# Split experts of a fused attention, gating and expert kernel: 32-bit parts, and scaled 16-bit parts with guards

## The chip, the cores and the metric

The kernel runs on one core of one Trainium2 chip. The metric is device time in microseconds (us) of one execution; of several runs the median is taken. A profile of one execution names the engines: PE is the matrix engine, PEld its loading of the stationary operand, DVE, ACT and POOL are the vector, scalar and general engines, and SP issues most of the DMAs.

## What is computed

Three stages follow one another: a linear attention with a decaying state (4 batches, 8 heads, 768 steps, 48 values), a dense stage with a gated soft activation and a layer norm (384 to 1024 to 384), and eight experts of which each token uses one.

```python
# stage 3, of which the change speaks: x is 3072 tokens by 384
logits = x @ w_gate                       # 8 experts
expert_idx = np.argmax(logits, axis=1)
gate_w = softmax(logits)[np.arange(N), expert_idx]
for e in range(8):
    mask = expert_idx == e
    h = np.maximum(x[mask] @ w1[e], 0.0)  # 384 to 1024
    out[mask] = gate_w[mask, None] * (h @ w2[e])   # 1024 to 384
```

## The kernel before

The tokens go in 24 tiles of 128. Each tile passes the attention (`square` to `yout`) and the dense stage (`ysquare` to `mm2`); then its rows are sent by an indirect DMA to the place of its expert in `xs` (`xrow`, `choose`, `gexp`, `gate`, `rank`, `place`, `send`). When nearly all tiles are sent, the experts run one after the other, each over as many rows as it may have: 480 (in two parts of 256 and 224 rows, y = 0 and 1, of the expert that leads after 15 tiles), then 464, 432, 416, 400, 384, 368 and 344.

Precision is kept by splitting: each operand is a high part and the rest, and three matmuls (high by high, high by rest, rest by high) stand for one. Of the attention's and the dense stage's second matmul the parts are 16 bits wide (`mm2`, line 567). Of the experts all parts are 32 bits wide (type F32R): the rows (`ehi` on ACT, `elo` on DVE, line 773 and 776), the weights (line 724 on ACT, 726 on DVE) and the inner values (`rhi` on ACT, line 800, `rlo` on DVE, line 803).

For one expert of n rows `emm1` (line 789) makes 72 matmuls of n columns, in four quarters of 18. After each quarter ACT takes the result to the high part (`hh`) and DVE to the rest (`hl`); the results stand in two large PSUM banks, so the third quarter needs the first one's bank back. The second layer is 72 matmuls of n columns where n is over 384 (`emm2t`, line 832), else 24 matmuls of 384 columns for each 128 rows (`emm2`, line 814). The two parts of the first expert have 72 matmuls each in `emm1` and 48 each in `emm2`. That is 648 matmuls at line 789, 288 at line 832 and 312 at line 814, together 1248. Between them stand 87 transposes of rows (`etrans`, line 770).

An expert's weights come in four chunks (1024, 512, 768 and 768 KB) through two staging buffers (`stage`, loads at line 717), and each chunk is split by ACT and DVE from there.

The order of the work is not written by hand: `plan()` takes every step with its engine, its cost and a due time from the table `X`, and always issues the step that can start first, among those within `EPS` of it the one with the lowest due time. Each engine then works through its own list strictly in that order. The steps of `tables()` (powers of the decay, needed by all attention steps) and the memsets around them stand ahead of that stretch and are ordered by the framework's scheduler.

At the end `marks`, `flags` and `judge` decide whether a slow path is needed (values out of the range that the split allows, or an expert with too many rows): `flags` is a small matmul, `judge` a chain on DVE whose last line (692) writes `fli`. All engines read `fli` (line 1206) and jump past the slow path.

Of the kernel before, what the change touches and what calls it, by code (L numbers as in the profile page):

```python
# [23 lines left out]
P = 128  # L24
# [9 lines left out]
NOID = 4095  # L34
SA, SV, SZ, SW = 2.0 ** 10, 2.0 ** 9, 2.0 ** 8, 2.0 ** 10
# [5 lines left out]
def body(ctx, tc, r, k, v, w, u, w_in, w_out, g_ln, w_gate, w1, w2, out):  # L41
# [18 lines left out]
    def sml(name, slot=None):  # L60
# [25 lines left out]
    X = dict(PK=14, ET=-29.23, GG=-120.46, SO=-383.87, FL=374.6, OL=1, ybuf=10, tmp=1, rkv=3, LAT=0.06,  # L86
             SELF=0.05, PRE=1.4, EPS=0.1, TA=176.56, TB=248.64, TM=254.17, NA=8, NB=9, M0=495.42, W0=42.93,
             TW=105, W1=-530.44, TV=257.99, PF=664.51, PW=-382.4, F0=-386.07, EL=3, e=3, S0=12.3, P0=10.1,
             D0=2.5, L0=-679.5, L1=615.58, U0=13.12, KG=9.92, PT=2, ZT=-247.56, F2=148.59, TE=84.91, GA=118.81,
             GW=-220.86, GN=157.31, DB=-1.5, KS=8.04, K0=610.2, K1=199.94, xtrans=-970.71, kev=571.15,  # L90
             ahi=622.76, vlo=9.17, ruk=307.19, attend=625.35, choose=-170.33, xhi=-20.99, vhi=706.01,
             own=263.22, hvar=668.67, hmax=132.27, gexp=-753.32, ktrans=-390.29, rtrans=539.68, hexp=150.63,
             ztrans=70.39, asum=173.22, rev=-2168.6, xlo=-650.67, decay=77.28, alo=655.25, rank=-472.96,
             ld=-228.91, xrow=-249.65, mm2=1203.62, causal=-107.84, hseed=-596.66, send=-284.2, hsolu=-201.28,
             yout=597.49, zlo=288.89, scores=540.82, square=141.08, place=-51.35, ysquare=-575.28,
             advance=-342.55, update=136.08, zscale=-399.78, hroot=-622.85, mm1=452.87, aval=631.76,
             kpow=460.49)
# [26 lines left out]
    thr = const.tile([P, 1], F32, name="thr")  # L124
    ph1 = ctx.enter_context(ExitStack())
# [447 lines left out]

    def choose(i):
# [100 lines left out]
    def judge():  # L675
# [15 lines left out]
        V.tensor_tensor(fl[:, 1:2], fl[:, 1:2], fl[:, 0:1], op=ALU.max)  # L691
        V.tensor_copy(fli[:, 1:2], fl[:, 1:2])
# [4 lines left out]
    wts = {}  # L697

    def weights(e):
# [3 lines left out]
        def pair(m):  # L703
            if m not in tiles:
                shape = [P, KD, FF] if m == 1 else [P, KF, DM]
                tiles[m] = [(wb if e % 2 else wa).tile(shape, F32R, name=f"w{m}{x}", tag=f"w{m}{x}") for x in "hl"]
            return tiles[m]

        def chunk(m, c0, n, width):
# [19 lines left out]
            return lambda part: split() if part else load()  # L729
# [3 lines left out]
    cv, sto, gt, wg, mxp = fold_pools(pha, "")  # L733
    tables()
# [29 lines left out]
    def etrans(d, c, slot=None):  # L764
        if c == 0:
            d["xh"] = d["new"]([P, KD, d["mx"]], F32R, "exh")[:, :, 0:d["nr"]]
            d["xl"] = d["new"]([P, KD, d["mx"]], F32R, "exl")[:, :, 0:d["nr"]]
# [161 lines left out]
    for i in range(NT):  # L929
# [49 lines left out]
        op(("choose", i), "", [("dve", .18), ("dve", .27), ("dve", .24), ("pool", .25)], [("mm2", i), ("send", i - 3), "wos"], choose, i, first=f + X["choose"])  # L979
        op(("xrow", i), "act", .58, [("mm2", i), ("send", i - 3), ("fill", E - 1), "wos"], xrow, i, first=f + X["xrow"])  # L980
# [28 lines left out]
    for y in range(E + 1):  # L1009
        e, d = max(y - 1, 0), {}  # L1010
        if y == 2:
            esends.clear()
        if y != 1:
# [4 lines left out]
            for n, (m, w_) in enumerate(((2, FF), (1, FF), (4, DM), (4, DM))):  # L1018
                op(("wload", e, n), "dma", m * w_ * 4 * P / 230e3, [("yout", NT - 1), ("who", 0)] + [("who", e), ("wlo", e, n - 2) if n > 1 else ("wlo", e - 1, n + 2), ("wload", e, n - 1) if n else ("wload", e - 1, 3)],
# [4 lines left out]
                   lambda g=wz[n]: g(1), first=f + X["GN"] * n)  # L1024
        f = start[y]
# [334 lines left out]
```

## Time and profile before

| what | value |
|---|---|
| median of 3 runs | 625.04 us (624.47 to 629.82) |
| the profiled execution's own time | 626.75 us |
| its span in the trace | 624.9 us |
[...]
| busy PE, PEld, DVE | 91%, 78%, 71% |
| busy ACT, POOL | 57%, 41% |

Times in the trace count from the span's start. "Busy" of PE holds the modelled end of each matmul, so that matmuls that follow closely show as one busy stretch; the pace is read from the distance between their starts. The chain of work that ended last is followed backwards from the last instruction, each piece to what released it.

### The profile page before, as it was taken

To read this page: it belongs to the slowest core of one execution; us is meant where nothing else is said; L and a number is where in the kernel's file an instruction comes from. 1 tells how busy PE (TensorE), PEld (TensorE's weight loads), DVE (VectorE), ACT (ScalarE), POOL (GpSimd) and SP (SyncE) were. 2 spreads that over 40 slices of the span, in tenths; PEclk is the share of its full clock that TensorE was granted. 3 is DMA by queue.
4 is the path that set the end of the run, shared out by engine and by line. 5 is a ranking of instruction groups with operands and counts; after the bars stand their busy time and mean duration, and the time that the engine had idled before them with its cause. 6 is when DMAs were issued, how large, how long until landed. Compare 5 with 4: busy or idle time off the path is not lost. (4 is left out here: it accounts for less than half of the span.)

```text
span 624.9 us, 10949 instructions
## 1 busy us (share of the span) xinstructions
PE 568.8 (91%) x4035; PEld 488.3 (78%) x4035; DVE 442.5 (71%) x781; ACT 354.8 (57%) x590; POOL 258.0 (41%) x427
## 2 busy tenths in 40 slices
PE   0757798999999999999999989999999999999990
PEld 0646687677777788878787658988899999989990
DVE  5899989978898989989877653537576767546211
ACT  2556677597688768678577762535252525345310
POOL 1687567365655646766543452110012121212210
PEclk9968799899999999999999999999999999999996
DMA  9736459794647475745324724853546585763100
GB/s 174 164 92 147 96 171 305 93 188 86 124 93 134 83 116 104 124 86 104 63 47 130 194 71 154 278 173 111 158 129 204 146 236 162 144 193 132 52 14 25
DMA packets 159872, 82.80 MB, mean 132 GB/s; under 512 B 136917, under 2 KB 153034, under 8 KB 159424
## 3 DMA queue, kind: packets, MB, share of 16 engines
q1 hardware_dynamic: 156544, 72.53, 50.9%
q0 software_dynamic: 3264, 9.47, 4.5%
q8 instruction: 34, 0.56, 0.4%
q14 instruction: 30, 0.25, 0.1%
HBM read 51.51 MB, written 16.12 MB: 108 GB/s over the span
## 5 line engine op out<-in xcount | busy, mean ns | idle before, releaser
L864 POOL DMA_INDIRECT out<-o,gt x29 | 34.5, 1190 | 196.4 <-ACT o L860 84.1
L567 PE MATMUL mm<-wo,zT 128*128 128x392 f16 x576 | 101.2, 333 | 2.3 <-DVE state L452 1.4
L482 PE MATMUL mm<-wi,xh 128*128 128x512 f32 x288 | 94.1, 409 | 0.6 <-DVE AT L409 0.6
L567 PEld LDWEIGHTS <-zT 128*128 128x128 f16 x576 | 55.8, 99 | 41.0 <-issue 2.3
L789 PE MATMUL emm<-exh,w1h 128*128 128x256 f32 (+8 forms) x216 | 72.4, 335 | 0.0
L789 PE MATMUL emm<-exl,w1h 128*128 128x256 f32 (+8 forms) x216 | 71.3, 330 | 0.0
L789 PE MATMUL emm<-exh,w1l 128*128 128x256 f32 (+8 forms) x216 | 71.3, 330 | 0.0
L800 ACT ACTIVATE hh<-emm 128x928 fp32r<-128x928 f32 (+8 forms) x32 | 27.6, 861 | 69.5 <-PE emm L789 58.1
L482 PEld LDWEIGHTS mm<-wi,xh 128*128 128x128 f32 x288 | 54.2, 194 | 11.4 <-DVE AT L409 0.8
L482 PE MATMUL mm<-wi,xl 128*128 128x512 f32 x144 | 57.6, 400 | 0.0
L803 DVE SCALAR_TENSOR_TENSOR hl<-emm,hh 128x928 fp32r<-128x928 f32 (+8 forms) x32 | 32.4, 1011 | 32.0 <-ACT hh L800 31.9
L726 DVE TENSOR_TENSOR w2l<-stage,w2h 128x768 fp32r<-128x768 f32 x32 | 30.1, 952 | 18.2 <-ACT w2h L724 18.2
L789 PEld LDWEIGHTS emm<-exh,w1h 128*128 128x128 f32 x216 | 40.8, 189 | 1.2 <-DVE hl L803 0.3
L789 PEld LDWEIGHTS emm<-exl,w1h 128*128 128x128 f32 x216 | 40.8, 189 | 0.8
L789 PEld LDWEIGHTS emm<-exh,w1l 128*128 128x128 f32 x216 | 40.7, 189 | 0.8
L621 POOL DMA_INDIRECT xs<-row,pos x24 | 28.1, 1172 | 27.2 <-issue 15.1
L726 DVE TENSOR_TENSOR w1l<-stage,w1h 128x1024 fp32r<-128x1024 f32 x24 | 28.9, 1221 | 13.0 <-ACT w1h L724 13.0
L528 ACT ACTIVATE e<-e,st 128x1024 f32<-128x1024 f32 x22 | 27.3, 1239 | 16.4 <-POOL st L524 16.4
L428 PE MATMUL attend<-sdec,rT 128*128 128x96 f32 x160 | 35.4, 307 | 0.0
L814 PE MATMUL emm<-w2h,hh 128*128 128x384 f32 (+3 forms) x104 | 35.2, 339 | 0.0
L814 PE MATMUL emm<-w2h,hl 128*128 128x384 f32 (+3 forms) x104 | 35.0, 337 | 0.0
L814 PE MATMUL emm<-w2l,hh 128*128 128x384 f32 (+3 forms) x104 | 35.0, 336 | 0.0
(216 smaller groups left out, 1546.4 us busy)
## 6 DMA issues: line engine op xcount, KB each, us to landing
stage<-in_moe_w SPq DMA_DIRECT2D x16, 768.0 KB, 6.3
stage<-in_moe_w SPq DMA_DIRECT2D x8, 1024.0 KB
xs<-zf SPq DMA_DIRECT2D x8, 772.0 KB, 10.4
rkv<-in_r SPq DMA_DIRECT2D x24, 192.0 KB, 4.0
rkv<-in_k SPq DMA_DIRECT2D x24, 192.0 KB, 5.0
rkv<-in_v SPq DMA_DIRECT2D x24, 192.0 KB, 4.5
stage<-in_moe_w SPq DMA_DIRECT2D x8, 512.0 KB, 4.2
xg<-xs SPq DMA_DIRECT2D x4, 772.0 KB, 6.5
```

Source lines behind the costliest of these rows:

```text
L428: T.matmul(ps[:, j * 96:j * 96 + 96], rT[:, j, :], sdec[:, j].rearrange("p a d -> p (a d)"), start=True, stop=False, skip_group_check=True)
L482: T.matmul(ps[:, n, :], a[:, j, :], wi[b][:, j, n * 512:(n + 1) * 512], start=(j == 0 and m == 0), stop=(j == KD - 1 and m == 2))
L528: A.activation(e, e, AF.Identity, scale=st[:, 10:11], bias=st[:, 11:12])
L567: T.matmul(ps[:, 0:OW], zz[:, a, c, :], wo[b][:, c, :], start=(c == 0 and m == 0), stop=(c == KF - 1 and m == 2))
L621: G.indirect_dma_start(out=xs, out_offset=bass.IndirectOffsetOnAxis(ap=pos.bitcast(U32), axis=0), in_=row, in_offset=None, bounds_check=E ...
L726: V.tensor_tensor(lo, d[:, x], hi.bitcast(F32), op=ALU.subtract)
L789: T.matmul(ps[:, x, :], a[:, j, fc * P:(fc + 1) * P], b[:, j, :], start=(j == 0 and m == 0), stop=(j == KD - 1 and m == 2))
L800: A.activation(cols(d, "hh", q), d["pm", q], AF.Relu)
L803: V.scalar_tensor_tensor(cols(d, "hl", q), d.pop(("pm", q)), 0.0, cols(d, "hh", q).bitcast(F32), op0=ALU.max, op1=ALU.subtract)
L814: T.matmul(ps[0:n, 0:DM], a[:, c, j * P:j * P + n], b[:, c, :], start=(c == 0 and m == 0), stop=(c == KF - 1 and m == 2))
L864: G.indirect_dma_start(out=out, out_offset=bass.IndirectOffsetOnAxis(ap=d["gt"][0:n, j, 1:2].bitcast(U32), axis=0), in_=d.pop(("o", j))[0: ...
```

## The change

Rows, weights and inner values of the experts become type F16. To keep them in range, rows are scaled by 256, the first weights by 16 and the second by 64; the gate's divisor takes the product, so the output is unscaled at no cost. The rest is now made by one `scalar_tensor_tensor` in place of one `tensor_tensor`.

New guards check that the 16 bits suffice. For each tile `xsq` squares the row on ACT and adds it up (24 instructions). For each chunk of weights `squares` does the same from the staging buffer (32 instructions of 2048, 1024, 1536 and 1536 elements); the next load into that buffer waits for it (`wsq`). The 34 instructions of `rhi` get an added sum. At the end `marks2` (DVE), `flags2` (PE) and `judge2` (DVE) join the new guards to the old ones; `judge` no longer writes `fli`, `judge2` does.

All due times in `X` are others, and the planner's costs of the experts' matmuls are lower (1.96 to 1.84, 2.62 to 2.46, 2.09 to 1.96, 1.05 to 0.99). The stretch of given order now begins ahead of `tables()`.

```diff
-    X = dict(PK=14, ET=-29.23, GG=-120.46, SO=-383.87, FL=374.6, OL=1, ybuf=10, tmp=1, rkv=3, LAT=0.06,
+    X = dict(GQ=247.24, xsq=-319.14, PK=14, ET=-237.63, GG=295.29, SO=306.5, FL=25.47, OL=1, ybuf=10, tmp=1,
...
+    def xsq(i):
+        sq = mid.tile([P, DM], BF16, tag="sqy", name="sqy", bufs=1)
+        A.activation(sq, tk["row", i][:, 0:DM], AF.Square, scale=SX, accum_out=g2sq[:, i:i + 1])
...
-        G.tensor_scalar(s[:, 2:3], s[:, 1:2], 1e-9, 1.0, op0=ALU.add, op1=ALU.mult)
+        G.tensor_scalar(s[:, 2:3], s[:, 1:2], 1e-9, SX * S1 * S2, op0=ALU.add, op1=ALU.mult)
...
+    def marks2():
+        n = NT + 4 * E
+        V.tensor_reduce(low[:, 0:1], hacc, op=ALU.max, axis=AX.X)
+        V.tensor_reduce(low[:, 1:2], g2sq[:, 0:n], op=ALU.max, axis=AX.X)
+        V.tensor_scalar(low[:, 0:1], low[:, 0:1], HMAX, None, op0=ALU.is_gt)
+        V.tensor_scalar(low[:, 1:2], low[:, 1:2], WMAX, None, op0=ALU.is_gt)
+        V.tensor_tensor(g2sq[:, n:n + 1], low[:, 0:1], low[:, 1:2], op=ALU.max)
+    def flags2(slot):
+        ps = tk["fl2"] = sml("flags2", slot)
+        T.matmul(ps[:, 0:NT + 4 * E + 1], mask, g2sq, start=True, stop=True)
+    def judge2():
+        ps, n = tk.pop("fl2"), NT + 4 * E
+        V.tensor_scalar(low[:, 0:NT], ps[:, 0:NT], XMIN, None, op0=ALU.is_lt)
+        V.tensor_scalar(low[:, NT:n], ps[:, NT:n], WMIN, None, op0=ALU.is_lt)
+        V.tensor_scalar(low[:, n:n + 1], ps[:, n:n + 1], 0.0, None, op0=ALU.is_gt)
+        V.tensor_copy(low[:, n + 1:n + 2], fl[:, 1:2])
+        V.tensor_reduce(fl[:, 1:2], low[:, 0:n + 2], op=ALU.max, axis=AX.X)
         V.tensor_copy(fli[:, 1:2], fl[:, 1:2])
...
-                    A.activation(hi, d[:, x], AF.Copy)
+                    A.activation(hi, d[:, x], AF.Copy, scale=(S1, S2)[m - 1])
-                    V.tensor_tensor(lo, d[:, x], hi.bitcast(F32), op=ALU.subtract)
+                    V.scalar_tensor_tensor(lo, d[:, x], (S1, S2)[m - 1], hi, op0=ALU.mult, op1=ALU.subtract)
...
+            def squares():
+                c = NT + 4 * e + 2 * (m - 1) + (c0 > 0)
+                A.activation(wsqt[0][:, 0:n * width], got[0][:, 0:n * width], AF.Square, scale=(S1, S2)[m - 1], accum_out=g2sq[:, c:c + 1])
...
+    man = tc.manual_schedule()
+    man.__enter__()
     tables()
...
-            d["xh"] = d["new"]([P, KD, d["mx"]], F32R, "exh")[:, :, 0:d["nr"]]
+            d["xh"] = d["new"]([P, KD, d["mx"]], F16, "exh")[:, :, 0:d["nr"]]
...
-                d[n] = d["new"]([P, KF, d["mx"]], F32R, n)[:, :, 0:d["nr"]]
-        A.activation(cols(d, "hh", q), d["pm", q], AF.Relu)
+                d[n] = d["new"]([P, KF, d["mx"]], F16, n)[:, :, 0:d["nr"]]
+        A.activation(cols(d, "hh", q), d["pm", q], AF.Relu, accum_out=hacc[:, 4 * d["y"] + q:4 * d["y"] + q + 1])
```

Three places show what the change does to the order. The first is DVE's list at the kernel's start: `tt`, `trT`, `rT` and `wdec` are the tables, `vl` is the rest part of the first tile's values. Before:

```order
L311 RECIPROCAL tt<-tt 128x4x9
L302 TENSOR_TENSOR tt<-tt 128x4
L378 SCALAR_TENSOR_TENSOR vl<-rkv_121,vh 128x384
L302 TENSOR_TENSOR tt<-tt 128x4
L303 RECIPROCAL tt<-tt 128x4
L324 TENSOR_TENSOR w_188<-tt 128x4
```

Now:

```order
L317 RECIPROCAL tt<-tt 128x4x16
L318 RECIPROCAL tt<-tt 128x4x9
L321 TENSOR_TENSOR rT<-tt 128x512
L321 TENSOR_TENSOR trT<-tt 128x512
L329 TENSOR_SCALAR trT<-trT 128x512
L331 TENSOR_TENSOR w_194<-tt 128x4
L332 MEMSET wdec 128x384
L334 COPY wdec<-w_194 64x4x48 x2
L385 SCALAR_TENSOR_TENSOR vl<-rkv_125,vh 128x384
```

The tile's `vl` stood in the middle of the tables and now stands behind all of them. On ACT at the same place (`tkm` is the table that PE's first transposes give, `sq` the guard's square of a tile) the list before was:

```order
L353 ACT_TABLE_LOAD
L353 ACTIVATE sq,guard<-rkv_121 128x1152
L374 ACTIVATE vh<-rkv_121 128x384
L353 ACTIVATE sq,guard<-rkv_122 128x1152
L321 ACTIVATE tkm<-tables 128x384
```

Now:

```order
L328 ACT_TABLE_LOAD
L328 ACTIVATE tkm<-tables 128x384
L381 ACTIVATE vh<-rkv_125 128x384
L360 ACTIVATE sq,guard<-rkv_125 128x1152
L381 ACTIVATE vh<-rkv_126 128x384
```

The table `tkm` now comes first, and the load of ACT's function table stands right ahead of it. On SP the decay's two small loads (`wc`) now stand ahead of the first tile's three, before they stood behind the first of them. On PE the first dense matmul (`mm1`) now stands behind six attention steps, before behind four.

The second place is ACT's list in the expert of 432 rows: `w1h` and `w2h` are the high parts of weights, `hh` the four quarters' inner values, `o` an output of the expert before, `wsq` a new square. Before:

```order
L724 ACTIVATE w2h<-stage 128x768 x4
L724 ACTIVATE w1h<-stage 128x1024 x2
L800 ACTIVATE hh<-emm_5441 128x2x432
L724 ACTIVATE w1h<-stage 128x1024
L800 ACTIVATE hh<-emm_5502 128x2x432
L800 ACTIVATE hh<-emm_5529 128x2x432
L724 ACTIVATE w2h<-stage 128x768
L773 ACTIVATE exh<-etrans 128x416 x3
L800 ACTIVATE hh<-emm_5553 128x2x432
```

Now:

```order
L757 ACTIVATE w1h<-stage 128x1024
L764 ACTIVATE wsq,g2sq<-stage 128x2048
L839 ACTIVATE hh,hacc<-emm_5535 128x2x432
L757 ACTIVATE w1h<-stage 128x1024 x2
L764 ACTIVATE wsq,g2sq<-stage 128x1024
L839 ACTIVATE hh,hacc<-emm_5563 128x2x432
L839 ACTIVATE hh,hacc<-emm_5591 128x2x432
L899 ACTIVATE o<-of,gt 128x384 x3
L899 ACTIVATE o<-of,gt 80x384
L839 ACTIVATE hh,hacc<-emm_5630 128x2x432
```

Squares stand directly ahead of the first and the second quarter's `hh`, and the outputs of the expert before ahead of the fourth.

The third place is the end of DVE's list, behind the last `hl`. Before:

```order
L677 COPY guard<-flags 128x24
L678 TENSOR_SCALAR guard<-flags 128x24
L679 TENSOR_REDUCE fl<-guard 128x1
L680 TENSOR_SCALAR fl<-fl 128x1
L681 TENSOR_TENSOR guard<-keys,kcap 128x8
L682 TENSOR_REDUCE fl<-guard 128x1
L684 TENSOR_TENSOR guard<-flags,eoff 128x8
L685 TENSOR_TENSOR keys<-flags,eoff 128x8
L686 TENSOR_SCALAR guard<-guard 128x8
L687 TENSOR_TENSOR guard<-guard,keys 128x8
L688 TENSOR_TENSOR guard<-guard,first_134 128x8
L689 TENSOR_REDUCE fl<-guard 128x1
```

Now (the first five wait for the last `hl` alone, the rest for PE's last matmul):

```order
L707 TENSOR_REDUCE low<-hacc 128x1
L708 TENSOR_REDUCE low<-g2sq 128x1
L709 TENSOR_SCALAR low<-low 128x1
L710 TENSOR_SCALAR low<-low 128x1
L711 TENSOR_TENSOR g2sq<-low 128x1
L719 TENSOR_SCALAR low<-flags_6934 128x24
L720 TENSOR_SCALAR low<-flags_6934 128x32
L721 TENSOR_SCALAR low<-flags_6934 128x1
L722 COPY low<-fl 128x1
L723 TENSOR_REDUCE fl<-low 128x1
L724 CAST fli<-fl 128x1
```

The old chain of `judge`, three more instructions long than shown, has moved to the beginning of the experts; behind PE's last matmul stand six instructions in place of 15.

## Rows read from the trace of the kernel before

**Rows 1.** Windows of the experts: busy PE, PEld, DVE, ACT, POOL, clock, DMA share, GB/s.

```profile
377.50:396.00 18.50, 18.49 (x135) 18.34 (x135) 5.67 (x21) 3.95 (x9) 3.74 (x8) 1.00 0.62 219
...
473.00:505.00 32.00, 32.00 (x174) 31.47 (x174) 20.78 (x25) 14.55 (x20) 6.70 (x5) 1.00 0.65 180
...
sum 233.00, PE 231.69 PEld 222.73 DVE 124.83 ACT 93.59 POOL 36.27; mean PE 25.74 PEld 24.75 DVE 13.87 ACT 10.40 POOL 4.03
```

**Rows 2.** The chain that ended last, experts: start us, us, what (224 to 464 columns).

```profile
377.70 4.40 PE emm L789 x36
...
396.75 8.07 PE emm L789 x72
...
415.09 15.26 PE emm L789 x72
430.35 10.06 PE emm L832 x48
...
449.21 12.52 PE emm L789 x63
...
562.91 10.92 PE emm L789 x63
...
586.42 11.47 PE emm L789 x72
597.89 12.57 PE emm L814 x72
```

**Rows 3.** Windows of the first stage: columns as in rows 1.

```profile
20.00:50.00 30.00, 19.17 (x183) 16.81 (x182) 28.23 (x29) 16.77 (x25) 24.78 (x17) 0.77 0.52 114
50.00:100.00 50.00, 42.33 (x323) 36.46 (x321) 46.72 (x58) 35.70 (x63) 34.02 (x33) 0.90 0.61 160
```

**Rows 4.** Timeline and page: 16-bit matmuls of 392 columns, start us, us.

```profile
354.68 4.15 PE L567 MATMUL mm<-wo,zT 128*128 128x392 f16 x24
...
L567 PE MATMUL mm<-wo,zT 128*128 128x392 f16 x576 | 101.2, 333 | 2.3 <-DVE state L452 1.4
```

**Rows 5.** The chain at the end: start us, us, what.

```profile
610.46 0.15 PE flags L671 x2
...
610.68 0.18 DVE guard L677
...
613.07 0.15 DVE fli L692
```

**Rows 6.** Timeline of the start: tables, their waits, first work of POOL.

```profile
6.03 0.10 DVE L302 TENSOR_TENSOR tt<-tt 128x4 f32<-128x4 f32 x1
...
7.62 1.28 ACT L353 ACT_TABLE_LOAD   x1 [7.62 <-DMA rkv<-in_v]
...
10.62 0.56 DVE L378 SCALAR_TENSOR_TENSOR vl<-rkv,vh 128x384 f16<-128x384 f32 x1 [4.48 <-ACT vh L374]
...
14.50 1.09 PE L320 MATMUL tables<-ident,rT 128*128 128x128 f32 x4 [14.50 <-DVE rT L314]
15.63 0.49 ACT L321 ACTIVATE tkm<-tables 128x384 f32<-128x384 f32 x1 [3.01 <-PE tables L320]
...
16.26 1.01 POOL L356 TENSOR_TENSOR kp<-rkv,tkm 128x384 f32<-128x384 f32 x1 [12.78 <-DMA raw<-in_moe_w_in]
```

**Rows 7.** Timeline of ACT: squares with a sum, and what starts next.

```profile
8.92 1.16 ACT L353 ACTIVATE sq<-rkv 128x1152 bf16<-128x1152 f32 x1
...
10.08 0.51 ACT L374 ACTIVATE vh<-rkv 128x384 f16<-128x384 f32 x1
...
339.55 0.51 ACT L459 ACTIVATE sqy<-av 128x384 bf16<-128x384 f32 x1
```

**Rows 8.** The page's groups of inner values, and the loads of weights.

```profile
L800 ACT ACTIVATE hh<-emm 128x928 fp32r<-128x928 f32 (+8 forms) x32 | 27.6, 861 | 69.5 <-PE emm L789 58.1
...
L803 DVE SCALAR_TENSOR_TENSOR hl<-emm,hh 128x928 fp32r<-128x928 f32 (+8 forms) x32 | 32.4, 1011 | 32.0 <-ACT hh L800 31.9
...
L717 SPq DMA_DIRECT2D stage<-in_moe_w x32: 345/373/1090, 334.3 to 569.7; - x32
```

More of the change, by code (lines that the diff above doesn't have):

```diff
@@ L84, in body @@
     V.memset(mhalf, -0.5)
-    X = dict(PK=14, ET=-29.23, GG=-120.46, SO=-383.87, FL=374.6, OL=1, ybuf=10, tmp=1, rkv=3, LAT=0.06,
[L87 to L97, printed above, removed]
@@ new lines, in body @@
+    X = dict(GQ=247.24, xsq=-319.14, PK=14, ET=-237.63, GG=295.29, SO=306.5, FL=25.47, OL=1, ybuf=10, tmp=1,
+             rkv=3, LAT=0.06, SELF=0.05, PRE=1.4, EPS=0.16, TA=168.5, TB=266.87, TM=311.03, NA=8, NB=9,
+             M0=743.86, W0=257.61, TW=424.23, W1=-271.89, TV=489.95, PF=102.61, PW=-27.68, F0=448.07, EL=3, e=3,
+             S0=12.3, P0=10.1, D0=2.5, L0=-559.91, L1=100.54, U0=-217.97, KG=30.69, PT=2, ZT=-320.39,
+             F2=-818.47, TE=55.36, GA=-1411.52, GW=-525.81, GN=483.04, DB=-1.22, KS=5.81, K0=327.85, K1=-222.09,
+             xtrans=-331.63, kev=79.89, ahi=-436.02, vlo=-467.16, ruk=10566.48, attend=956.32, choose=321.9,
+             xhi=-554.14, vhi=1071.76, own=14.4, hvar=352.35, hmax=214.2, gexp=-149.89, ktrans=-349.49,
+             rtrans=527.68, hexp=516.67, ztrans=-122.83, asum=-72.01, rev=-87.83, xlo=-250.39, decay=484.11,
+             alo=869.91, rank=-98.93, ld=170.93, xrow=263.31, mm2=1671.9, causal=-76.96, hseed=-1632.59,
+             send=-141.07, hsolu=482.26, yout=-863.09, zlo=-412.45, scores=14.94, square=1438.13, place=-633.36,
+             ysquare=371.5, advance=-1129.74, update=896.02, zscale=527.22, hroot=-719.47, mm1=533.9,
+             aval=2371.65, kpow=69.68)
@@ L1024, in body @@
                    lambda g=wz[n]: g(1), first=f + X["GN"] * n)
+                op(("wsq", e, n), "act", m * w_ / 1024 * 1.0 + .24, [("wload", e, n)], lambda g=wz[n]: g(2), first=f + X["GN"] * n + X["GQ"])
         f = start[y]
@@ L1040, in body @@
         for q in range(nq):
-            op(("em1", y, q), "", [("pe", 1.96 * ks if wide else 1.05)] * nx, got + [("wlo", e, 0), ("wlo", e, 1)] + ([("em1", y, q - 1)] if q else []),
+            op(("em1", y, q), "", [("pe", 1.84 * ks if wide else .99)] * nx, got + [("wlo", e, 0), ("wlo", e, 1)] + ([("em1", y, q - 1)] if q else []),
                lambda slot, d=d, q=q: emm1(d, q, slot), bank="b", until=[("rlo", y, q)], first=f + 3.7 * q)
-            op(("rhi", y, q), "act", .97 * ks, [("em1", y, q)] + [("em2", y - 1, j) for j in range(4)], lambda d=d, q=q: rhi(d, q), first=f + 3.7 * q)
+            op(("rhi", y, q), "act", .2 + .97 * ks, [("em1", y, q)] + [("em2", y - 1, j) for j in range(4)], lambda d=d, q=q: rhi(d, q), first=f + 3.7 * q)
             op(("rlo", y, q), "dve", 1.15 * ks, [("rhi", y, q)], lambda d=d, q=q: rlo(d, q), first=f + 3.7 * q)
@@ L1047, in body @@
             for j in range(KD):
-                op(("em2", y, j), "", [("pe", 2.62 * ks)] * 2, [("rlo", y, q) for q in range(nq // 2)] + [("wlo", e, 2)],
+                op(("em2", y, j), "", [("pe", 2.46 * ks)] * 2, [("rlo", y, q) for q in range(nq // 2)] + [("wlo", e, 2)],
                    lambda slot, d=d, j=j: emm2t(d, j, slot), then=[("rlo", y, q) for q in range(nq // 2, nq)] + [("wlo", e, 3)], bank="s", until=[("osp", y, j)], first=fo + 4.8 * j)
@@ L1062, in body @@
             for j in range(nt):
-                op(("em2", y, j), "", [("pe", 2.09)] * 2, [("rlo", y, q) for q in range(nq // 2)] + [("tail", y), ("wlo", e, 2)],
+                op(("em2", y, j), "", [("pe", 1.96)] * 2, [("rlo", y, q) for q in range(nq // 2)] + [("tail", y), ("wlo", e, 2)],
                    lambda slot, d=d, j=j: emm2(d, j, slot), then=[("rlo", y, q) for q in range(nq // 2, nq)] + [("wlo", e, 3)], bank="s", until=[("eout", y, j)], first=f + 3.7 * nq + 3.9 * j)
@@ L1068, in body @@
                 esends.append(("esend", y, j))
+    op("marks2", "dve", .8, ["marks", "judge"] + [("rhi", y, q) for y in range(E + 1) for q in range(4)] + [("wsq", e, n) for e in range(E) for n in range(4)] + [("xsq", i) for i in range(NT)], marks2, first=0)
+    op("flags2", "pe", .3, ["marks2"], flags2, bank="s", until=["judge2"], first=0)
+    op("judge2", "dve", 1.0, ["flags2"], judge2, first=0)
     PORT = {"vlo", "zlo", "bits", "wil", "wol", "alo", "decay", "kpow", "ruk", "aval"}
@@ L1172, in close_a @@
         stage = ph2.enter_context(tc.tile_pool(name="stage", bufs=2, side="right", reuse_waits="tile"))
+        wsqt.append(stage.tile([P, 2048], BF16, tag="wsq", name="wsq", bufs=1))
         e0 = ph3.enter_context(tc.tile_pool(name="e0", bufs=1, side="right", reuse_waits="tile"))
```

31 lines of the change are left out of this document (19 added, 12 removed).

## The prediction

> **What bounds the kernel now.** I read the busy shares by stretch first, then the chain that ended last, then the timelines of the places that the change touches. [...]
>
> **The experts' matmuls: -17.5 us.** The chain gives the pace for each width, as length by count [rows 2]: 224 columns 112.1 ns (8.07/72), 256: 122.2 (4.40/36), 344: 159.3, 368: 173.3, 432: 198.7, 464: 211.9. [...] The 87 transposes stay 32 bits wide and keep their time. [...]
>
> **The end: -1.5 us.** Before, the chain on DVE behind PE's last matmul runs from 610.68 to 613.22, 15 instructions [rows 5]. Now six stand there, the first three without dependence on one another: three starts 0.1 us apart, then copy, reduction and cast at about 0.2, some 1.0 us. `marks2` needs only the last `hl`, which is done about 11 us before PE's end, and `judge` itself has moved to the first expert. The jump and the closing instructions keep their time.
>
> **The start: -3 us.** The tables' chain on DVE stops at 6.13 us for 4.48 us, since `vl` stands in its middle and waits for ACT; ACT's own list waited until 7.62 us for a load [rows 6]. Now `vl` stands behind the tables, and the small load of the decay goes first on SP. PE's first transposes, at 14.50, can then begin 4.48 + 0.56 us earlier. Against it, the function table's load of 1.28 us now lies between them and `tkm`, where before it was long done: net 3.8 us for POOL's first product at 16.26. The row after that load shows the square 0.02 us behind its end (7.62 + 1.28 and 8.92) [rows 6, 7]. [...] I take 3 of the 3.8 us: the first 100 us are bound by DVE, so an earlier DVE moves the rest along, but the list is also sorted anew, with six attention steps ahead of the first dense matmul in place of four. What that alone can do has no row; PE is idle for 18.5 us of 20 to 100 [rows 3], and I let the re-sorting cost up to 5 us or gain up to 9.
>
> **The squares and sums on ACT: +4 us.** A square of 1152 elements takes 1.16 us until the next instruction starts, one of 384 elements 0.51 [rows 7]: 0.846 ns an element, so 1.92, 1.05 and twice 1.48 us for a set of weights, 5.9 us. Eight sets are 47.4 us, the 34 sums of `rhi` at about 0.1 us 3.4, the 24 squares of rows 12 us. ACT's 94 us of 233 become about 138 of 215 [rows 1]; the average covers it. What it does not cover is order: ACT waited 58 us in all for PE's quarters [rows 8], so it stood ready when a quarter was done. Now squares stand directly ahead of some `hh`. [...] I take half a microsecond for each of the eight sets, 4 us, between nothing and the full 50.8 us of squares of weights and sums. The 12 us for rows lie in a stage that PE bounds and are taken at nothing; the splits on DVE become instructions like `vl`, 0.56 us for 384 elements with a 16-bit result [rows 6], and I take them as long as before, on an engine that is idle for half of this stage; the loads are the same.
>
> **The sum.** -17.5 - 1.5 - 3 + 4 = -18.0 us. Against the profiled execution's own 626.75 that is 608.75; the median of the runs stands 1.7 lower, so 607.05, and I say 607 us. What a measurement of this kernel can tell from no change is about 1%, 6.25 us.
>
> **Rivals.**
> 1. *The start gains more.* If the re-sorted first stage uses half of PE's idle time there, the gain is 9 us beside the 3, and 598 us come out. For it: DVE is full and PE is not [rows 3]. Against it: the dense stage's first matmul is later in the list.
> 2. *Weights come late.* The next load into a staging buffer waits for the square. Before, 32 loads start from 334.3 to 569.7 us, one in 7.6 us [rows 8], and the second layer of the last expert begins at 597.89 [rows 2], so the last chunk lands and is split some 15 us ahead. With two buffers each round grows by a square, 1.5 us in the mean, 0.74 a load, over 28 loads 21 us; less the 3 of the start the last load starts at 587, lands 6 us later and is split by 597. PE, which would be there at 580, then waits for about half of the second layer, and ends some 7 us later than the rest of the sum: 614 to 620, say 617 us. Against it: the loads before were spaced by their due times and not by full buffers.
> 3. *Slower: the squares are in the way.* ACT takes its list strictly in order, so a `hh` behind a square and behind the load that the square waits for is late in every quarter, PE waits for the bank, and the loads slip too. At three quarters of 50.8 us exposed, 626.75 - 22.0 + 38 - 1.7 = 641 us. It decides from the point at which 22.0 of the 50.8 us, 43%, are exposed. For it: the new list of the 432-row expert has squares ahead of two quarters and outputs ahead of the fourth. Against it: ACT idled for 60% of this stage. [...]
> [...]
>
> **How the numbers follow.** The forecast has 0.68 (its own range 601 to 614: squares from nothing to 10 us, start from 0 to -6), the first rival 0.14, the second 0.09, the third 0.06, the fourth 0.03. Faster by over 1% are the forecast, the first and half of the second: 0.87; within 1% the rest of the second, the fourth and a little of the third: 0.08; slower 0.05. The range from 597 to 618 leaves out the third and fourth, and parts of the others.
>
> **What would show it.** Right: the starts of the 464-column matmuls lie 196 ns apart, of the 344-column ones 146; PE stays busy for over 97% of the experts' stage, which takes about 216 us; the chain behind the last matmul is near 1.1 us; POOL's first product comes near 12.5 us. Wrong: gaps of PE behind `hh` or `hl` at the third quarter of an expert (rival 3), ACT waiting for the staging loads late in the stage (rival 2), a pace above 200 ns at 464 columns (rival 4), or an experts' stage that begins more than 5 us from 374 (the start).

## The result and the profile after

The changed kernel takes 618.95 us in the median (618.07 to 619.19, 3 runs) against 625.04: a ratio of 0.9884, with a 95% interval from 0.9839 to 0.9929. That is 6.1 us, where 18.0 were forecast; 607 us and the range from 597 to 618 both missed it. Measured once more beside the experiments below it took 616.8 us, a ratio of 0.9858 (0.9773 to 0.9943); that lies just inside the range, at about half of the gain that was forecast.

The profiled executions differ by 7.4 us of span (624.9 to 617.5). Read by three marks, the balance is: the first matmul of the experts begins 2.3 us later (377.6 to 379.9), the experts' stage takes 224.4 in place of 232.5 us, and the tail from PE's last expert matmul to the span's end 13.2 in place of 14.8 us: +2.3 - 8.1 - 1.6 = -7.4.

The page of the changed kernel: busy shares, the chain that ended last by engine, and the group of the new squares.

```profile
PE 561.5 (91%) x4037; PEld 405.3 (66%) x4037; DVE 441.4 (71%) x776; ACT 417.4 (68%) x734; POOL 266.5 (43%) x443
...
DMA 10%; issue 9%; PE 3%; ACT 1%; DVE 0%; POOLq 0%; POOL 0%; ACTq 0%
...
L764 ACT ACTIVATE wsq<-stage 128x1536 bf16<-128x1536 f32 (+2 forms) x32 | 47.2, 1476 | 0.0
```

The squares of weights are 47.2 us, as estimated (47.4). The chain that ended last has changed its nature: before it was mostly matmuls [rows 2], with sends of output rows as 7% of the span; now the sends are its largest part and PE has 3%.

Windows of the changed kernel (columns as in [rows 1]; the first two answer to [rows 3], the last to the sum of [rows 1], the two between are the dense stage and its end):

```profile
20.00:50.00 30.00, 21.91 (x192) 19.45 (x192) 28.29 (x30) 20.16 (x34) 25.03 (x17) 0.70 0.72 154
50.00:100.00 50.00, 45.02 (x383) 40.09 (x382) 45.38 (x55) 34.59 (x61) 35.63 (x35) 0.84 0.66 142
...
120.00:340.00 220.00, 215.81 (x1733) 167.19 (x1732) 184.90 (x360) 176.13 (x326) 128.76 (x259) 1.00 0.57 106
340.00:380.00 40.00, 33.24 (x200) 20.63 (x198) 20.09 (x62) 30.01 (x59) 20.49 (x60) 0.96 0.32 84
...
379.90:604.60 224.70, 218.51 (x1338) 134.89 (x1337) 126.61 (x179) 135.81 (x224) 31.28 (x35) 0.98 0.51 158
```

In the experts' stage PE is busy for 218.5 of 224.7 us at a granted clock of 0.98; in [rows 1] it was 231.7 of 233.0 at 1.00. So two things are new there: 6.2 us of idle PE in place of 1.3, and stretches at a granted clock of 0.5. In the dense stage and its end PE is idle for 4.2 and 6.8 us; before, the same two windows had none and 3.6:

```profile
120.00:340.00 220.00, 220.00 (x1818) 172.27 (x1817) 187.10 (x379) 164.74 (x297) 129.14 (x263) 1.00 0.57 105
340.00:380.00 40.00, 36.43 (x227) 24.96 (x225) 24.12 (x71) 25.31 (x48) 19.09 (x56) 1.00 0.43 119
```

**The start** came out better than computed. The timeline of the changed kernel, against [rows 6]:

```profile
0.80 1.28 ACT L328 ACT_TABLE_LOAD   x1 [0.80 <-PEq L1392]
...
8.20 1.09 PE L327 MATMUL tables<-ident,rT 128*128 128x128 f32 x4 [8.20 <-DVE rT L321]
...
9.33 0.49 ACT L328 ACTIVATE tkm<-tables 128x384 f32<-128x384 f32 x1 [7.24 <-PE tables L327]
...
9.96 2.35 POOL L363 TENSOR_TENSOR kp<-rkv,tkm 128x384 f32<-128x384 f32 x2 [6.42 <-ACT tkm L328]
```

PE's first transposes come at 8.20 in place of 14.50 and POOL's first product at 9.96 in place of 16.26. That is 6.3 us earlier, not 3.8. Half of the difference is the function table's load: it stands first in ACT's list, waits for no data and was done at 2.1 us, so its 1.28 us never came between the transposes and `tkm`. The other half is that the transposes came 6.3 us earlier and not 5.04.

**The end** came out as computed. The timeline behind the last matmul, against [rows 5]:

```profile
604.44 0.33 PE L715 MATMUL flags<-g2sq,mask 128*128 128x57 f32 x2
...
604.80 0.18 DVE L719 TENSOR_SCALAR low<-flags 128x24 f32<-128x24 f32 x1 [9.53 <-PE flags L715]
...
605.49 0.15 DVE L724 CAST fli<-fl 128x1 int32<-128x1 f32 x1
```

From 604.80 to 605.64 it is 0.84 us, six instructions; before, 2.54.

**The experts** lost their time at about three quarters of the stage. First ACT's list there (`o` are rows to be sent out, L899 those of the 400-row expert, L859 those of the 384-row one; L757 splits the next weights); then PE's list at the same place.

```profile
541.41 2.13 ACT L899 ACTIVATE o<-of,gt 128x384 f32<-128x384 f32 x4
549.19 0.58 ACT L859 ACTIVATE o<-emm,gt 128x384 f32<-128x384 f32 x1 [5.65 <-DMA out<-o,gt]
549.66 0.83 ACT L757 ACTIVATE w2h<-stage 128x768 f16<-128x768 f32 x1
...
561.03 0.58 ACT L859 ACTIVATE o<-emm,gt 128x384 f32<-128x384 f32 x1 [4.58 <-DMA out<-o,gt]
561.51 0.83 ACT L757 ACTIVATE w2h<-stage 128x768 f16<-128x768 f32 x1
562.24 0.77 ACT L839 ACTIVATE hh<-emm 128x736 f16<-128x736 f32 x1
```

```profile
550.07 0.80 PE L809 MATMUL etrans<-ident,xg 128*128 128x128 f32 x6
553.22 0.54 PE L809 MATMUL etrans<-ident,xg 128*128 128x128 f32 x3 [2.35 <-ACT o L859]
...
555.39 0.51 PE L828 MATMUL emm<-exh,w1h 128*128 128x368 f16 x1
555.70 0.51 PE L828 MATMUL emm<-exl,w1h 128*128 128x368 f16 x1
...
557.90 0.32 PE L828 MATMUL emm<-exh,w1h 128*128 128x368 f16 x1
558.06 0.32 PE L828 MATMUL emm<-exl,w1h 128*128 128x368 f16 x1
...
564.22 0.32 PE L828 MATMUL emm<-exh,w1h 128*128 128x368 f16 x1 [1.95 <-DVE hl L842]
```

Four outputs made in a row at 541.41 fill the four buffers that outputs have. The fifth, at 549.19, waits 5.65 us until the first of them has been sent and has landed, and the seventh 4.58 us for the third. ACT took its list in order there: the splits of the next weights, a square and `hh` stand behind these waits, each split follows 0.47 or 0.48 us behind the start of the output that waited, and PE waits 2.35 and 1.95 us. From 555.39 the matmuls of 368 columns start 0.31 us apart and from 557.90 0.16: the granted clock was 0.5 from 554.2 to 557.6 us, and 1.00 from 557.8.

The buffers come back slowly because the sends go one at a time: POOL begins the next only when the one before has landed. First one of POOL's rows, then pieces of the chain that ended last (start, us from issue to landing):

```profile
526.03 0.97 POOL L903 DMA_INDIRECT out<-o,gt  x1 [2.38 <-DMA out<-o,gt]
```

```profile
522.67 2.57 DMA out<-o,gt
...
526.03 4.16 DMA out<-o,gt
...
542.30 6.78 DMA out<-o,gt
...
553.21 7.80 DMA out<-o,gt
```

The send of 542.30 landed at 549.08, just ahead of the fifth output, and that of 553.21 at 561.01, just ahead of the seventh. `plan()` reckons 1.04 us on POOL and 2.4 us more for a send (line 1100 of the changed kernel), 3.4 us where these two took 6.78 and 7.80. The kernel before had such waits too, with both splits of `w2h` ahead of them; there they were 2.94, 2.78 and 0.43 us, and PE lost 1.3 us by them:

```profile
558.40 0.58 ACT L820 ACTIVATE o<-emm,gt 128x384 f32<-128x384 f32 x1 [2.94 <-DMA out<-o,gt]
```

**The end of the dense stage** has a similar place: the timeline of ACT, DVE and PE where the last tiles (`z`, `zT`) meet the first expert's weights.

```profile
345.45 1.23 ACT L535 ACTIVATE e<-e,st 128x1024 f32<-128x1024 f32 x1
346.58 0.83 ACT L757 ACTIVATE w2h<-stage 128x768 f16<-128x768 f32 x1
347.32 1.47 ACT L764 ACTIVATE wsq<-stage 128x1536 bf16<-128x1536 f32 x1
...
349.85 1.04 ACT L537 ACTIVATE z<-e 128x1024 f16<-128x1024 f32 x1
...
350.93 1.23 DVE L541 TENSOR_TENSOR z<-e,z 128x1024 f16<-128x1024 f32 x1 [0.24 <-ACT z L537]
...
356.55 5.67 PE L574 MATMUL mm<-wo,zT 128*128 128x392 f16 x24 [2.70 <-DMA zT<-z]
```

`e` is done at 346.7, but `z` starts at 349.85 behind weights and a square; the tile then goes over DVE and a DMA, and PE waits until 356.55. Its 24 matmuls of 392 columns take 5.67 us here against 4.15 in [rows 4], because the granted clock was 0.5 from 356.3 to 359.7.

### The profile page after: what moved, and what is told of

It is laid out like the page before. It is cut to its first block, busy times and chain, and to the rows that moved or that the text cites. A ratio compares the mean times of both kernels' runs of the same rounds, so it can differ in the third digit from the quotient of the medians.

```text
span 617.5 us, 11075 instructions
## 1 busy us (share of the span) xinstructions
PE 561.5 (91%) x4037; PEld 405.3 (66%) x4037; DVE 441.4 (71%) x776; ACT 417.4 (68%) x734; POOL 266.5 (43%) x443
## 5 line engine op out<-in xcount | busy, mean ns | idle before, releaser
L828 PE MATMUL emm<-exh,w1h 128*128 128x256 f16 (+8 forms) x216 | 70.0, 324 | 1.9 <-DVE hl L842 1.9
L828 PE MATMUL emm<-exl,w1h 128*128 128x256 f16 (+8 forms) x216 | 69.9, 324 | 0.4 <-DVE exl L815 0.4
L828 PE MATMUL emm<-exh,w1l 128*128 128x256 f16 (+8 forms) x216 | 69.9, 324 | 0.0
L828 PEld LDWEIGHTS <-w1h 128*128 128x128 f16 x432 | 42.6, 100 | 27.0 <-issue 2.8
L842 DVE SCALAR_TENSOR_TENSOR hl<-emm,hh 128x928 f16<-128x928 f32 (+8 forms) x32 | 32.2, 1010 | 36.9 <-ACT hh L839 36.6
L759 DVE SCALAR_TENSOR_TENSOR w2l<-stage,w2h 128x768 f16<-128x768 f32 x32 | 30.2, 954 | 26.7 <-ACT w2h L757 26.7
L764 ACT ACTIVATE wsq<-stage 128x1536 bf16<-128x1536 f32 (+2 forms) x32 | 47.2, 1476 | 0.0
L412 PE MATMUL scores<-rT,kT 64*128 64x128 f32 x384 | 31.8, 313 | 11.2 <-DVE rT L399 7.8
L541 DVE TENSOR_TENSOR z<-e,z 128x1024 f16<-128x1024 f32 x22 | 30.9, 1403 | 7.8 <-ACT z L537 7.7
L853 PE MATMUL emm<-w2h,hh 128*128 128x384 f16 (+3 forms) x104 | 33.9, 326 | 0.0
```

What stands on the lines that cost most here:

```text
L412: T.matmul(ps[:, a, j * P:(j + 1) * P], kT[h, j, :], rT[h, j, :], start=True, stop=True)
L541: V.tensor_tensor(z[:, 1, :], tk.pop(("e", i)), z[:, 0, :], op=ALU.subtract)
L759: V.scalar_tensor_tensor(lo, d[:, x], (S1, S2)[m - 1], hi, op0=ALU.mult, op1=ALU.subtract)
L764: A.activation(wsqt[0][:, 0:n * width], got[0][:, 0:n * width], AF.Square, scale=(S1, S2)[m - 1], accum_out=g2sq[:, c:c + 1])
L828: T.matmul(ps[:, x, :], a[:, j, fc * P:(fc + 1) * P], b[:, j, :], start=(j == 0 and m == 0), stop=(j == KD - 1 and m == 2))
L853: T.matmul(ps[0:n, 0:DM], a[:, c, j * P:j * P + n], b[:, c, :], start=(c == 0 and m == 0), stop=(c == KF - 1 and m == 2))
```

## The experiments

Three theories stood. *Order*: the new lists (due times) cost what the types gain. *Squares*: the guards' instructions on ACT cost it. *Next limit*: with faster matmuls, DVE and ACT end last whatever the list. Each median is from 4 runs unless another count is given; the kernel before ran beside them at 626.3, 626.9 and 626.3 us (experiments 1 to 4, 5 to 8, 9 to 12). A difference of 2 or 3 us between two of these medians is near what they can tell; where a smaller one is used, it is read from stages of the traces. Each stage is one trace's; the two traces of the changed kernel differ by 1.3 us in the experts' stage (224.4 and 223.1, experiment 12), so a difference of that size in a stage shows little by itself.

**1. The types alone, in the old list.**

```diff
-            d["xh"] = d["new"]([P, KD, d["mx"]], F32R, "exh")[:, :, 0:d["nr"]]
+            d["xh"] = d["new"]([P, KD, d["mx"]], F16, "exh")[:, :, 0:d["nr"]]
...
-                    A.activation(hi, d[:, x], AF.Copy)
+                    A.activation(hi, d[:, x], AF.Copy, scale=(S1, S2)[m - 1])
...
-        G.tensor_scalar(s[:, 2:3], s[:, 1:2], 1e-9, 1.0, op0=ALU.add, op1=ALU.mult)
+        G.tensor_scalar(s[:, 2:3], s[:, 1:2], 1e-9, SX * S1 * S2, op0=ALU.add, op1=ALU.mult)
```

and so for the other parts.

> The kernel before with the 16-bit types and scales alone: its due times, its order on every engine, no guards. Theory 'order' (the new list costs what the types gain) and theory 'squares' (the guards' instructions on ACT cost it): the whole 17.5 us of pace come out, 625.0 - 17.5 = 607.5 us, the experts' stage from first to last matmul 232.5 - 17.5 = 215 us. Theory 'next limit' (with faster matmuls DVE's and ACT's work between the quarters is what ends last, whatever the list): only about 9 of the 17.5 us, as in the changed kernel, 614 to 617 us, with PE idle in the middle of the experts' stage.

Measured: 609.6 us, ratio 0.9761 (0.9702 to 0.9820). The experts' stage takes 216.8 us (375.7 to 592.5). The types are worth 16.7 us in a list that had been sorted for 32 bits; *next limit* falls. Its stage and a piece of its chain, the last expert's first layer of 344 columns:

```profile
375.70:592.70 217.00, 214.15 (x1334) 132.86 (x1334) 124.39 (x160) 93.45 (x135) 35.59 (x34) 1.00 0.54 165
```

```profile
570.58 10.50 PE emm L789 x72
```

10.50/72 = 145.8 ns, as forecast (146).

**2. The changed kernel without squares and sums.**

```diff
-        A.activation(sq, tk["row", i][:, 0:DM], AF.Square, scale=SX, accum_out=g2sq[:, i:i + 1])
-                A.activation(wsqt[0][:, 0:n * width], got[0][:, 0:n * width], AF.Square, ...)
-        A.activation(cols(d, "hh", q), d["pm", q], AF.Relu, accum_out=hacc[...])
+        A.activation(cols(d, "hh", q), d["pm", q], AF.Relu)
```

> The changed kernel without the 24 squares of rows, the 32 squares of weights and the 34 sums of the inner values (the guards' sums are set to a harmless constant, nothing else is left out); every other instruction stands where it stood on its engine. Theory 'squares': the experts' stage falls from 224.4 to about 216 us and the time from 619 to 609 to 611 us. Theory 'order': the waits remain, 616 to 619 us. Theory 'next limit': 616 to 619 us.

Measured: 613.8 us; the experts' stage 221.6 us, the first expert at 377.5. That is between the theories: 2.8 us of the stage and 2.4 us ahead of it come back, not 8. ACT's first wait for a buffer stays (5.40 us), while PE's wait behind `hl` near 564 us is gone.

**3. The same with 32-bit parts.** Experiment 2 with

```diff
-            d["xh"] = d["new"]([P, KD, d["mx"]], F16, "exh")[:, :, 0:d["nr"]]
+            d["xh"] = d["new"]([P, KD, d["mx"]], F32R, "exh")[:, :, 0:d["nr"]]
```

and so for all parts; scales kept.

> The run before (no squares, no sums, the changed kernel's list) with the experts' parts 32 bits wide again, scales kept. Theory 'squares': pace alone differs, 17.5 us above the run before, about 627 us. Theory 'order': the list's waits are hidden behind slower matmuls, so less than 17.5 us above the run before: 627 to 631 us, and above the kernel before by what the list costs with 32 bits, 2 to 6 us. Theory 'next limit': 9 us above the run before, 626 to 628 us.

Measured: 628.4 us (10 runs), ratio 1.0026 (0.9996 to 1.0056); the experts' stage 235.6 us. The whole time lies in or beside the ranges of all three theories; it is that of the kernel before, although the tables come early and the end is short. The stages say more: the new list costs 3.1 us of the stage at 32 bits (235.6 against 232.5) and 4.8 at 16 (221.6 against 216.8), with no square in it. So the list costs time by itself, as *order* has it. That it costs more beside faster matmuls (the types are worth 14.0 us here and 15.7 in the old list) is within what two traces can differ.

**4. Eight out buffers.**

```diff
-        d["o", j] = d["new"]([P, DM], F32, "o", 4)
+        d["o", j] = d["new"]([P, DM], F32, "o", 8)
```

> The changed kernel with eight buffers for the rows that an expert sends out in place of four; the list of every engine is the same. In the changed kernel ACT waits up to 5.7 us for such a buffer, near 553 us, with the splits of the next weights behind it. Theory 'order' in the form 'an output placed ahead of its buffer holds ACT up': those waits go, 615 to 617 us. Theory 'squares' and theory 'next limit': the waits are not what sets the time, 618 to 619 us.

Measured: 612.4 us, ratio 0.9767 (0.9714 to 0.9820), more than expected. The experts' stage falls from 224.4 to 218.2 us with the same list and all guards. ACT's list at the same place:

```profile
540.88 2.13 ACT L899 ACTIVATE o<-of,gt 128x384 f32<-128x384 f32 x4
545.84 0.58 ACT L859 ACTIVATE o<-emm,gt 128x384 f32<-128x384 f32 x1 [2.83 <-PE emm L853]
546.32 0.83 ACT L757 ACTIVATE w2h<-stage 128x768 f16<-128x768 f32 x1
```

The fifth output now waits for PE's result alone and comes 3.35 us earlier, and the split behind it too; the second wait, 4.58 us, is gone, and with it the granted clock of 0.5 at that place: the matmuls of 368 columns start 0.16 us apart from 551.96 to 555.86.

**5. Tables inside the stretch, old list, 16 bits, no guards.** Experiment 1 with

```diff
+    man = tc.manual_schedule()
+    man.__enter__()
     tables()
...
-    man = tc.manual_schedule()
-    man.__enter__()
     for t, _, key, slot in order:
```

> The first run (list of before, 16-bit types alone) with the stretch of given order beginning ahead of the tables, as in the changed kernel; everything behind the tables in the old order. In the changed kernel PE's first transposes came 6.3 us earlier, and the first expert 2.3 us later. Theory 'the new due times lost it' (matmuls of the first layer drawn ahead, the second layer's left as a chain of waits at the end of the dense stage): with the old list the gain arrives, the first expert's matmuls begin at 370 us in place of 375.7, 603 to 605 us against 609.6. Theory 'the dense stage takes it back' (DVE and PE bound the first 100 us whatever the tables do): the first expert begins at 374 to 376, 608 to 610 us.

Measured: 606.6 us, ratio 0.9669 (0.9614 to 0.9724). PE's tables are 6.3 us earlier (14.4 to 8.1), the first expert 2.1 (375.7 to 373.6), the median 3.1 us lower. Both theories are half right: the dense stage takes back two thirds, and the rest arrives. From 120 to 340 us PE has no idle time in this run:

```profile
120.00:340.00 220.00, 220.00 (x1818) 172.56 (x1816) 186.57 (x380) 165.28 (x298) 130.16 (x265) 1.00 0.57 106
340.00:380.00 40.00, 36.43 (x245) 25.40 (x244) 23.71 (x69) 23.42 (x41) 18.93 (x53) 1.00 0.42 117
```

**6. Eight buffers and no squares.** Edits of 2 and 4 together.

> The changed kernel with eight out buffers and without squares and sums (the guards' sums set to a constant), every other instruction in place. Theory 'two costs' (the squares take ACT's time by themselves, the buffers hold ACT up by themselves): the gains add, 612.4 - 5.0 = 607.4 us, the experts' stage at 218.2 - 2.8 = 215.4 us. Theory 'one cost' (both only shorten the same delay of the next weights' split near 550 us): no more than the eight buffers alone, 611 to 612.5 us.

Measured: 610.9 us. The experts' stage takes 218.0 us, against 218.2 with the squares: with buffers enough the 32 squares of weights and 34 sums cost nothing that a trace can tell (0.2 us), where with four buffers they cost 2.8. "One cost" holds there: the squares only lengthen the delays behind the outputs that wait. The first expert begins at 376.7 in place of 379.4.

**7. The changed kernel with its tables outside again.** The edit of 5 turned round.

> The changed kernel with the tables ahead of the stretch of given order again, as in the kernel before; due times, types and guards stay. Theory 'the start's gain is lost on the way' (the dense stage's end is a chain of waits that begins from DMAs and ACT and not from the start): 618 to 621 us, the first expert's matmuls at 379 to 382. Theory 'the start is worth its time' (without it the new due times would be still worse): 622 to 625 us, the first expert at 383 to 386.

Measured: 621.4 us (9 runs), ratio 0.9904 (0.9877 to 0.9931), between the two theories: by the medians the early tables are worth 2.4 to 4.6 us in the new list too. (The profiled execution of this kernel lay 5 us above its median, so its stages are not used.)

**8. All parts in the old list.** The due times and costs of before, eight out buffers; squares put into it by hand (the lines for the loads are left out here):

```diff
-    X = dict(GQ=247.24, xsq=-319.14, PK=14, ...
+    X = dict(PK=14, ET=-29.23, ...
...
+        if key[0] == "wlo":
+            due.append(key[1:])
+        if due and (key == "marks2" or o["eng"] == "act" and (key[0] == "rhi" or False)):
+            sqs[due.pop(0)]()
+        if key[0] == "gexp":
+            xsq(key[1])
```

> All parts of the change, but in the old order: due times of before, tables inside the stretch, eight out buffers, each square of weights put behind the next 'hh' on ACT or ahead of the load that needs its buffer, each square of rows behind its tile's exponential. Theory 'order': the guards cost ACT little where it idles, 604 to 608 us, 11 to 15 us under the changed kernel. Theory 'squares': wherever they stand they cost 3 to 5 us: 607 to 612 us. Theory 'next limit': 612 us or more.

Measured: 609.1 us, ratio 0.9723 (0.9668 to 0.9779). The first expert begins at 372.7 us and the experts' stage takes 215.9. But the old list has `judge` behind the last matmul, so that PE waited 3.2 us there for the joined flags: the tail is 16.5 us. By its whole time alone this run would fit *squares* (607 to 612); the stage and the tail say that it is the flags, and the next run tries that.

**9. The same with the flags earlier.**

```diff
-    X = dict(PK=14, ET=-29.23, GG=-120.46, SO=-383.87, FL=374.6, ...
+    X = dict(PK=14, ET=-29.23, GG=-120.46, SO=-383.87, FL=250, ...
```

> The run before it (old list, all parts, eight out buffers, tables inside the stretch) with the old flags and their judgement given an earlier due time, so that they stand ahead of the last expert's second layer. In that run PE waited 3.21 us behind its last matmul for them and the new guards. If the chain behind the last matmul counts in full, as the prediction's term of the end has it: 609.1 - 3.3 = 605.8 us, 605 to 607, with 13 us from PE's last expert matmul to the span's end in place of 16.5. If the earlier flags push something else away on DVE or PE: 608 to 610 us.

Measured: 606.2 us, ratio 0.9684 (0.9624 to 0.9744), the fastest kernel with all parts, inside the range of *order* for the run before it; the tail is 12.6 us. Its windows (dense stage, its end, experts) and two pieces of its chain, of 464 and 384 columns:

```profile
120.00:340.00 220.00, 220.00 (x1816) 173.07 (x1815) 188.72 (x378) 172.92 (x330) 132.52 (x271) 1.00 0.57 108
340.00:380.00 40.00, 35.82 (x228) 23.75 (x226) 22.42 (x66) 27.91 (x55) 17.48 (x47) 0.91 0.34 101
...
373.60:590.00 216.40, 214.38 (x1338) 133.13 (x1337) 127.13 (x185) 139.94 (x228) 36.95 (x33) 1.00 0.52 163
```

```profile
422.03 9.42 PE emm L871 x48
...
556.00 11.70 PE emm L853 x72
```

ACT carries all squares (139.9 us of 216.4, 46 more than in experiment 1) and PE is as busy as there.

**10. The old list with four out buffers.** Experiment 8 with the buffers of before.

> The old list with all parts and tables inside the stretch, but four out buffers as in the kernel before and the changed one. Theory 'order' (it is the place of the outputs in the new list, ahead of the splits of the next weights, that makes the wait for a buffer cost PE): the old list waits as little as before, 609 to 611 us against 609.1 with eight buffers, the experts' stage 216 to 218 us. Theory 'buffers' (with 16-bit matmuls four buffers are too few in any list): 613 to 616 us, the experts' stage 220 to 222 us.

Measured: 610.0 us, the experts' stage 217.9 us. *Order* holds: in this list four buffers cost 2.0 us of the stage, in the new one 6.2. ACT's list at the place:

```profile
537.61 1.12 ACT L899 ACTIVATE o<-of,gt 128x384 f32<-128x384 f32 x2 [2.08 <-DVE of L893]
...
540.11 1.10 ACT L899 ACTIVATE o<-of,gt 128x384 f32<-128x384 f32 x2
541.12 1.56 ACT L757 ACTIVATE w2h<-stage 128x768 f16<-128x768 f32 x2
...
545.92 0.58 ACT L859 ACTIVATE o<-emm,gt 128x384 f32<-128x384 f32 x1 [1.32 <-DMA out<-o,gt]
```

The four outputs go out in two pairs, from 537.61 on, and both splits of `w2h` stand ahead of the output that waits, which waits 1.32 us. A second thing differs: the first two of these sends landed after 2.6 and 4.0 us, in the changed kernel after 6.8 and 2.6. Which of the two spares the time was not tried apart; in experiment 1 the four outputs stand in one row as in the changed kernel, with `w2h` ahead of the outputs that wait, and the longest wait is 2.93 us.

**11. Eight buffers, without the squares of rows alone.** The first edit of experiment 2 with that of 4.

> The changed kernel with eight out buffers and without the 24 squares of rows (their sums set to a constant); squares of weights and sums of inner values stay, and every other instruction keeps its place. With all guards left out as well the first expert began at 376.7 in place of 379.4 us. Theory 'rows': the squares of rows on ACT at the dense stage's end cost this, 376.7 us, 609.5 to 611 us in all. Theory 'first weights': it is the squares of the first expert's weights, ahead of the dense stage's last tiles on ACT: the first expert stays at 379.4, 612 to 613 us.

Measured: 610.4 us, the first expert at 375.8. PE in the dense stage is busy for 217.53 of 220 us, as with all guards left out (217.40 in experiment 6), and 215.83 with them (experiment 4; 216.70 in experiment 12):

```profile
120.00:340.00 220.00, 217.53 (x1747) 167.69 (x1746) 185.13 (x365) 166.30 (x293) 127.71 (x266) 1.00 0.57 109
```

So it is the squares of rows that cost time in the new list: 1 to 2 us of the dense stage, 2.1 with its end (PE is idle for 8.8 us from 120 to 380 in place of 10.9), and 3.6 by the start of the first expert. The intervals of the two whole times overlap.

**12. The changed kernel again**, unedited.

> The changed kernel once more, beside the others on the same chip. All theories: 618 to 620 us, a ratio to the kernel before of 0.986 to 0.992.

Measured: 616.8 us (615.2 to 623.3), the first expert at 379.8, the experts' stage 223.1 us: as in the first measurement, within a microsecond or two.

## Why the prediction was wrong

Against the profiled executions, -18.0 us were forecast and -7.4 measured. Of the 10.6 us between them 5.4 lie in the experts' stage (-17.5 + 4 forecast, -8.1 measured) and 5.3 ahead of it (-3 forecast, +2.3 measured); the end gives 0.1 back.

**Pace: right.** 464 columns are 196.3 ns apart (9.42/48 in experiment 9) where they were 209.6 (10.06/48), 384 columns 162.5 (11.70/72) where they were 174.6 (12.57/72), 344 columns 145.8 (10.50/72 in experiment 1) where they were 159.3 (11.47/72) [rows 2]: 13.3, 12.1 and 13.5 ns less. The 16-bit matmuls of the dense stage had shown such a pace, (4.15 - 0.33)/23 = 166.0 ns for 392 columns [rows 4]. No run shows the clock rate behind the forecast of -17.5 us; what the runs show are these paces, and at 32 bits (211.9 - 112.1)/240 = 0.416 ns for each column between 224 and 464 [rows 2]. In the old list the types bring 15.7 of 17.5 us in the experts' stage.

**End: right** (-1.5 forecast, -1.6 measured).

**Squares, "+4 us": ACT's list was priced by the wrong instructions.** What the stage lost against the forecast pace is 224.4 - 215.0 = 9.4 us. Eight buffers give back 6.2 of it (experiment 4), leaving the guards out 2.8 (2), both together 6.4 (6). So these are not two costs that add: outputs wait for one of four buffers with splits behind them, and in this stage the guards cost time only where that happens. Of the 3.0 us that are left, 1.8 are missing in the old list too, with the types alone (216.8); the other 1.2 are too small for these traces to place. The step that failed is "now squares stand directly ahead of some `hh`" as the only thing on ACT to be priced. The prediction saw "outputs ahead of the fourth" quarter under rival 3 and gave them no price of their own; it never asked what those outputs wait for. No run shows the half microsecond for each set of which the +4 us were made: with four buffers the guards cost 2.8 us of the stage (2), with eight 0.2 (6). That 2.8 is near 4 is luck: the squares in the 432-row expert cost nothing, since PE was busy for all 30.1 us of that expert (445.8 to 475.9) at a granted clock of 1.00. ACT's load was forecast well (138 of 215 us, its terms without the first expert's squares, which lie ahead of the stage; 139.9 of 216.4 in experiment 9), but load was not the question.

**Start, "-3 us": the right size by luck, and the new list left at nothing.** Alone, the early tables bring 3.1 us (5 against 1). But the prediction had 3.8 us at POOL's first product and let 3 of them through; there were 6.3, and 2.1 came through to the first expert. Two errors cancelled. The step that failed is "I let the re-sorting cost up to 5 us or gain up to 9", with nothing taken for it: in the new list the first expert begins at 379.9 us, in the old one with early tables at 373.6, 6.3 us apart. By the windows PE is idle 10.95 us from 120 to 380 in place of 3.57. "The 12 us for rows [...] are taken at nothing" failed with it: 2 to 4 us in the new list (11), while in the old one with all squares the first expert began at 372.7 and 373.6 us (8, 9). Which of the due times does the rest was not tried apart, so that cause stays open; the rows at 345 to 357 us show one such place.

**Signs.** "PE stays busy for over 97% of the experts' stage" came true (218.5 of 224.7 us) in a stage that had lost 9 us: a matmul at a granted clock of 0.5 is busy for longer (0.51 us at 368 columns, against 0.32 at 1.00). The "about 216 us" beside it are the pace without the prediction's own +4, which make 219. A gap of PE behind `hl` at the third quarter, the sign of rival 3, was there in the expert of 368 rows (564.22); it is gone without the squares (2) and also with eight buffers (4). The experts' stage began 5.9 us from 374, beyond the 5 that were named as a sign of being wrong.

**Rivals.** The third had the right kind of cause, ACT's list taken in order, mostly in other instructions and at four times the size. The second (late weights) did not occur: PE's waits in the experts' stage are for outputs and rest parts, none for a load of weights. (Its price is not the sum that it gives: 7 us on 607 make 614, and 617 needs 10.) The whole forecast of 607 us would have fitted the same parts in the old list (606.2, though with eight buffers).

## What to carry to other kernels

When a change brings a new order with it, price the order by itself: an instruction that waits for a buffer is charged with what its engine has behind it in the list (here splits, a square and `hh` behind waits of 5.65 and 4.58 us on ACT, and then 2.35 and 1.95 us of PE), and beside faster matmuls such waits counted for more here (in the old list the same waits of ACT, up to 2.9 us, cost PE 1.3 us beside 32-bit matmuls and 2.3 beside 16-bit ones). Before trusting a busy share, look for outputs that leave in bursts as large as their buffer pool, and for how many of their sends run at once; doubling the pool here was worth as much as removing all the added work (612.4 and 613.8 us). And keep the old order as a candidate: here the new types, guards and early start, put into it by hand with the larger pool, beat the re-sorted kernel by 1.7% (606.2 against 616.8 us). With eight buffers in both lists it is 1.0% (606.2 against 612.4), which the intervals of these runs do not quite separate.

## What was not expected of the hardware

Some short waits of PE were followed by slower matmuls. In the changed kernel, between 340 us and the experts' last matmul, the granted clock fell to 0.5 three times, for 3.4 us from 356.3, 380.1 and 554.2 us, so that 24 matmuls that take 4.15 us in [rows 4] took 5.67. Shortly ahead of each PE had waited twice, 1.44 and 2.70, 1.21 and 1.19, 2.35 and 0.44 us; behind the single wait of 1.95 us that ended at 564.2 the clock stayed at 1.00. What makes it fall is not shown.

A send of 128 output rows by POOL landed between 2.6 and 7.8 us after its issue, and the next began only behind it. The two longest near 550 us ran while the DMA engines moved 204 and 162 GB/s, one of 2.6 us between them while they moved 76; but two others of 2.6 us ran at over 200 GB/s (from 564.64 and 576.74), so what makes a send long is not shown. So the burst of four outputs from 541.41 was drained by four sends in a row, begun at 542.30, 549.86, 553.21 and 561.81 us, and the two longest of them, 6.78 and 7.80 us, are what the pool of four buffers did not cover.
